# A layer-norm, attention and MLP kernel: the first 512 tokens of its head worked in two halves, and one V tile's products placed on both sides of the next chunk's transposes

## The chip, the cores and the metric

The kernel runs on one core of one Trainium2 chip. The metric is the device time of one launch in microseconds (us), as the median of several runs.

## What is computed

The input x has 2048 tokens of 512 features. It is layer-normed, and two branches read the result: attention with 32 heads of 16, and a gated MLP of inner width 1376.

```python
xn = _layernorm(x, axis=-1)                     # (x - mean) / sqrt(var + 1e-5)
qkv = xn @ wqkv                                 # q, k, v of 32 heads of 16
s = softmax(q @ k.T * 16 ** -0.5) @ v @ wo      # by head
g = silu(gelu(xn @ w1 + b1) @ w2 + b2)
return x + s * g
```

Each float32 operand of a product is split into a high part, rounded to the type that TensorE (PE) reads, and a low part, the rest. A product is the sum of three: high by high, high by low and low by high.

## The kernel before

The tokens are 16 tiles of 128 and 4 chunks of 512 (`NT`, `NCH`, `CH`); the features are 4 blocks of 128 (`KT`). The instructions of each engine stand in the order in which the Python code issues them (`manual_schedule`); each engine works its own list in order and waits for the others by semaphores. So the order of the code is the order of work, and an instruction that waits holds back all that stand behind it on its engine.

The part of the program that concerns us is its head, which prepares the operands. For a chunk, `ln` calls three steps on VectorE (DVE): `moments` of each tile (statistics and their aggregate, L414 and L415), `rstd` of the chunk (epsilon L419, the square root on ScalarE (ACT) at L420, the reciprocal and one refining step L421 to L424), and `norm` of each tile (L428), which also asks for the x tile six places on. `turn` transposes a normed tile on PE (L437, four blocks into one PSUM bank), and `split` takes the bank apart: ACT writes the high part (L86), DVE the low part (L87). The high and low parts of x lie in `slot0` and `slot1` for chunk 0, `slot2` and `slot3` for chunk 1, and so on.

`q_first(c)` makes the q and k rows of the first two head groups for a chunk: 24 products of 512 columns (L455) in two groups of accumulation, each in a bank of its own. They go term by term (high by high, then high weight by low x, then low weight by high x), and within each term first group 0, then group 1. `evac` then copies both banks (ACT, L370), splits them (ACT L374, POOL L375) and writes them to scratch memory. `v_tile(t)` makes the V rows of one token tile with 12 products (L92 by way of `mm3`), and `v_out` copies them into `vsb` on ACT (L387). V's weights are split on ACT (`wv_h`, L511) and POOL (`wv_low`, L502). Before the second pair of low halves, POOL waits in `pool_after` (L499) for a given normed tile.

Banks come from `a_tile`, which counts its calls and hands out six in turn: `ps_b`, `ps_x`, two of `spare` (shown as `sp`), `ps_t` (shown as `pst`) and `ps_a`. All of `ps_a`, `ps_b` and `ps_x` are shown as `ps`. A bank taken for the second time makes PE wait until whatever read its former contents is done.

The order of the head's code is: 25 warming products of the identity (`keep_warm`, L487), moments, root and norms of chunk 0, the split of the q and k weights (`w_split`, L294 on ACT, L295 on POOL), the transposes of tiles 0 to 3, `q_first(0)`; and then for each chunk c from 1: the transposes of its four tiles, `ln` of chunk c + 1, `v_tile(c - 1)` and `q_first(c)`. `ln` of chunk 1 is issued ahead of `q_first(0)`. Since `ln` of chunk c + 1 is issued ahead of `v_tile(c - 1)`, its square root stands on ACT ahead of that tile's `v_out`.

Behind the head come the MLP with the scores for the row maxima and then the attention itself (its first products with V in the chain of waits are at 484.65 us); their order is fixed as well.

Of the kernel before, what the change touches and what calls it, by code (L numbers as in the profile page):

```python
# [16 lines left out]
P = 128  # L17
S = 2048
D = 512
H = 32  # L20
DH = 16
KT = D // P
NT = S // P
CH = 512
# [30 lines left out]
def fused(ctx: ExitStack, tc: tile.TileContext, x, wqk, wv, wo, w1, b1, w2, b2, out):  # L55
# [308 lines left out]
    def evac(us, ph):  # L364
        raws = [wk.tile([P, CH], F32, name="hg", bufs=2) for u in us]
        for u, raw in zip(us, raws):
            if u[0] == "m":
                nc.scalar.activation(raw, ph.pop(u), AF.Gelu_apprx_tanh, bias=b1_sb[:, u[2]:u[2] + 1])  # L368
            else:
                nc.scalar.activation(raw, ph.pop(u), AF.Copy)  # L370
        for u, raw in zip(us, raws):
            hh = wk.tile([P, CH], F32R, name="hh", bufs=HB)
            hl = wk.tile([P, CH], F32R, name="hl", bufs=HB)
            nc.scalar.activation(hh, raw, AF.Copy)  # L374
            nc.gpsimd.tensor_sub(hl, raw, hh.bitcast(F32))  # L375
            if u[0] == "m":
                HS[u[1:]] = (hh, hl)
            else:
                rs, cs = slice(u[1] * P, (u[1] + 1) * P), slice(u[2] * CH, (u[2] + 1) * CH)
                nc.sync.dma_start(qk_h[rs, cs], hh.bitcast(F32))  # L380
                nc.sync.dma_start(qk_l[rs, cs], hl.bitcast(F32))
# [3 lines left out]
    def v_out(t, pv):  # L385
        dst = vsb[:, t, :H * VW].rearrange("p (h w) -> p h w", w=VW)[:, :, :DH]
        nc.scalar.activation(dst, pv.rearrange("p (h w) -> p h w", w=DH), AF.Copy)  # L387

    with ExitStack() as s1:
# [4 lines left out]
        def a_tile(shape):  # L394
            banks[0] += 1
            i = banks[0] % 6
            if i < 3:
                return (ps_a, ps_b, ps_x)[i].tile(list(shape), F32, name="ps")
            return f_bank(shape)
# [12 lines left out]
        def moments(t):  # L412
            st = w1k.tile([P, 6], F32, name="st")
            nc.vector.bn_stats(st, xs[t])  # L414
            nc.vector.bn_aggr(mv[:, t, :], st)  # L415

        def rstd(t0, t1):
            v = ve[:, :, t0:t1]
            nc.vector.tensor_scalar(v[:, 0], mv[:, t0:t1, 1], EPS, None, op0=OP.add)  # L419
            nc.scalar.activation(v[:, 1], v[:, 0], AF.Sqrt)  # L420
            nc.vector.reciprocal(v[:, 2], v[:, 1])  # L421
            nc.vector.scalar_tensor_tensor(v[:, 3], v[:, 2], -0.5, v[:, 2], op0=OP.mult, op1=OP.mult)
            nc.vector.tensor_mul(v[:, 3], v[:, 3], v[:, 0])
            nc.vector.scalar_tensor_tensor(v[:, 4], v[:, 3], 1.5, v[:, 2], op0=OP.add, op1=OP.mult)  # L424
# [8 lines left out]
        def turn(t):  # L433
# [4 lines left out]
            c, ts = t // NCH, slice(t % NCH * P, t % NCH * P + P)  # L438
            split(xh[c][:, :, ts], xl[c][:, :, ts], pt)

        def v_tile(t):
            pv = a_tile((P, D))
            c, ts = t // NCH, slice(t % NCH * P, t % NCH * P + P)
            for k in range(KT):
                mm3(pv, (xh[c][:, k, ts], xl[c][:, k, ts]), (wv_h[:, k], wv_l[:, k]), k == 0, k == KT - 1)
            v_out(t, pv)

        def q_first(c):
            pq = {}
            for n, (i, j) in enumerate(((0, 0), (0, 1), (1, 0))):  # L450
                for g in range(2):
                    if n == 0:
                        pq["q", g, c] = a_tile((P, CH))
                    for k in range(KT):
                        nc.tensor.matmul(pq["q", g, c], W1[g][i][:, k * P:(k + 1) * P], (xh, xl)[j][c][:, k],  # L455
                                         start=n == 0 and k == 0, stop=n == 2 and k == KT - 1)
            evac(list(pq), pq)

        for t in range(4):
            load_x(t, (nc.sync, nc.scalar)[t % 2])  # L460
# [24 lines left out]
        def keep_warm(n):  # L485
            for _ in range(n):
                nc.tensor.matmul(pw[:, :P], ident, ident, start=True, stop=True)  # L487

        keep_warm(25)
        def ln(t, n):  # L490
            for i in range(t, t + n):
                moments(i)
            rstd(t, t + n)
            for i in range(t, t + n):
                norm(i)

        ln(0, NCH)
        def pool_after(t):
            nc.gpsimd.tensor_sub(warm[:, :1], xns[t][:1, :1], xns[t][:1, :1])  # L499

        def wv_low(k):
            nc.gpsimd.tensor_sub(wv_l[:, k], wv_r[:, k], wv_h[:, k].bitcast(F32))  # L502

        pool_after(NCH - 1)
        for g in range(2):
            W1[g] = w_split(W1[g], "w1", 4)
        for t in range(NCH):
            turn(t)
        keep_warm(3)
        for k in range(KT):  # L510
            nc.scalar.activation(wv_h[:, k], wv_r[:, k], AF.Copy)  # L511
        for k in range(KT - 2):
# [3 lines left out]
        pool_after(2 * NCH - 1)  # L516
        for k in range(KT - 2, KT):
            wv_low(k)
        q_first(0)
        for c in range(1, NCH):  # L520
            for t in range(NCH * c, NCH * c + NCH):
                turn(t)
            if c < NCH - 1:
                ln(NCH * c + NCH, NCH)
            else:
                nc.scalar.activation(warm[:, 1:], warm[:, :1], AF.Gelu_apprx_tanh)
                break
            v_tile(c - 1)
            q_first(c)

    keep_r = ctx.enter_context(tc.tile_pool(name="keep_r", bufs=1, side="right"))
# [549 lines left out]
```

## Time and profile before

| | |
|---|---|
| median of 3 runs | 1546.86 us (1546.65 to 1547.5) |
| profiled execution | 1546.35 us, span 1544.6 us |
| busy PE / DVE / ACT / POOL | 100% / 92% / 78% / 24% |
| granted clock of PE | 1.00 |
| first statistics on DVE | 3.89 us |
| first q, k products on PE | 11.94 us |
| first transposes of chunk 1 | 18.11 us |
| q, k products of chunk 1 begin | 22.74 us |
| first transposes of chunk 2 | 28.34 us |
| first product of the MLP part | 51.49 us |

Times in the table's lower half are counted from the start of the span. In a timeline each row is a run of like instructions on one engine: start, length, engine, line, what is written from what, shapes and count, and in brackets how long the engine stood idle just before and which engine's work ended that. PE's products overlap, so the length of a row of products holds the tail of the last; the pace is read from start to start.

### The profile page before, as it was taken

How to read it: one execution, taken by the hardware profiler on the slowest of the kernel's cores; microseconds unless marked ns; L12 is line 12 of the kernel's file. 1: busy time of each engine (PE TensorE's matmuls, PEld its weight loads, DVE VectorE, ACT ScalarE, POOL GpSimd, SP SyncE). 2: the span in 40 equal slices, each digit the busy share in tenths (PEclk: the TensorE clock that was granted, in tenths of full speed). 3: DMA queues.
4: the chain of work that ended last, by engine and by line, in shares of the span. 5: the costliest groups of instructions: out<-in, count | busy, mean ns of one | idle time of the engine just before them, and what ended most of it. 6: DMA issues, size and time to landing. Idle time of an engine off the chain costs nothing.

```text
span 1544.6 us, 31302 instructions
## 1 busy us (share of the span) xinstructions
PE 1538.4 (100%) x12230; PEld 922.5 (60%) x12230; DVE 1419.2 (92%) x2294; ACT 1212.4 (78%) x1881; POOL 375.8 (24%) x386
## 2 busy tenths in 40 slices
PE   9999999999999999999999999999999999999998
PEld 8899999999995444444444444444444444444456
DVE  7799999999998999999999999999999999999945
ACT  4333433333339999999999999999999999999994
POOL 4235575756741011001000100100010000000153
PEclk9999999999999999999999999999999999999999
DMA  6615443455422112112411411411051111110162
GB/s 212 155 58 145 124 143 108 120 161 136 141 90 66 39 45 61 33 37 51 75 28 33 71 33 41 60 44 29 21 84 29 32 32 30 41 32 20 50 217 100
DMA packets 78227, 116.83 MB, mean 76 GB/s; under 512 B 28132, under 2 KB 28388, under 8 KB 76904
## 3 DMA queue, kind: packets, MB, share of 16 engines
q1 hardware_dynamic: 73596, 99.80, 23.1%
q0 software_dynamic: 4000, 14.45, 5.0%
q8 instruction: 96, 1.57, 0.4%
q10 hardware_dynamic: 484, 0.60, 0.1%
q14 instruction: 51, 0.42, 0.1%
HBM read 84.35 MB, written 25.97 MB: 71 GB/s over the span
## 4 chain that ended last, share of the span: by engine, by line
PE 99%; DVE 1%; DMA 0%; issue 0%; ACT 0%; DVEq 0%
PE pv L787 33%; PE ps L193 22%; PE ps L583 13%; PE two L716 8%; PE sp L583 5%; PE ps L716 4%; PE pst L716 4%; PE pst L583 3%; PE pv L583 2%; PE ps L916 2%; PE ps L92 1%; PE ps L455 1%; PE pst L92 0%; DVE st L414 0%; PE two L92 0%; DMA xt<-in_x 0%
## 5 line engine op out<-in xcount | busy, mean ns | idle before, releaser
L199 DVE TENSOR_REDUCE mx<-ps 128x2 f32<-128x512 f32 x2048 | 1318.0, 687 | 68.5 <-PE ps L193 18.3
L787 PE MATMUL pv<-slot,vsb 128*32 128x512 f32 x4096 | 543.4, 604 | 0.0
L721 ACT ACTIVATE slot<-two 128x1024 f32<-128x1024 f32 x511 | 520.5, 1019 | 0.0
L193 PEld LDWEIGHTS ps<-kt,slot 48*128 48x128 f32 x1356 | 212.2, 184 | 290.2 <-DVE mx L199 278.4
L193 PE MATMUL ps<-kt,slot 48*128 48x256 f32 (+1 forms) x1356 | 376.3, 366 | 0.0
L719 ACT ACTIVATE slot<-ps 128x512 f32<-128x512 f32 x515 | 307.5, 598 | 16.7 <-PE ps L716 7.2
L719 ACT ACTIVATE slot<-pst 128x512 f32<-128x512 f32 x511 | 309.9, 606 | 0.0
L583 PE MATMUL ps<-slot,w1h 64*128 64x512 f32 x1088 | 225.4, 392 | 0.0
L193 PE MATMUL ps<-kt,qz 48*128 48x512 f32 x512 | 202.2, 395 | 0.0
L716 PE MATMUL two<-qt,kt 50*128 50x512 f32 x766 | 197.5, 395 | 0.3 <-DVE gt L643 0.3
L716 PE MATMUL ps<-qt,kt 50*128 50x512 f32 x387 | 189.7, 492 | 0.0
L193 PEld LDWEIGHTS ps<-slot,slot 48*128 48x128 f32 x590 | 92.8, 184 | 124.0 <-DVE mx L199 118.2
L193 PE MATMUL ps<-slot,slot 48*128 48x256 f32 (+1 forms) x590 | 165.8, 366 | 0.0
L787 PEld LDWEIGHTS pv<-slot,vsb 128*32 128x32 f32 x4096 | 81.5, 108 | 131.9 <-issue 124.4
L583 PEld LDWEIGHTS ps<-slot,w1h 64*128 64x128 f32 x1088 | 154.1, 185 | 9.8
L583 PE MATMUL ps<-slot,w1l 64*128 64x512 f32 x544 | 157.0, 392 | 0.0
L716 PE MATMUL pst<-qt,kt 50*128 50x512 f32 x383 | 155.7, 406 | 0.0
L375 POOL TENSOR_TENSOR hl<-hg,hh 128x512 fp32r<-128x512 f32 x76 | 96.7, 1295 | 158.2 <-ACT hh L374 109.3
L368 ACT ACTIVATE hg<-ps,b_sb 128x512 f32<-128x512 f32 x44 | 27.9, 684 | 133.0 <-PE ps L583 121.7
L716 PEld LDWEIGHTS two<-qt,kt 50*128 50x128 f32 x766 | 114.5, 186 | 1.1 <-DVE gt L643 0.7
L246 POOL CAST mh<-nt 128x32 fp32r<-128x32 f32 x19 | 4.0, 209 | 375.7 <-DVE nt L244 322.8
L193 PEld LDWEIGHTS ps<-kt,qz 48*128 48x128 f32 x512 | 93.7, 183 | 1.0 <-DVE mx L199 0.7
(197 smaller groups left out, 1974.6 us busy)
## 6 DMA issues: line engine op xcount, KB each, us to landing
raw<-in_w SPq DMA_DIRECT2D x88, 256.0 KB
qk_h<-hh SPq DMA_DIRECT2D x32, 256.0 KB
qk_l<-hl SPq DMA_DIRECT2D x32, 256.0 KB
qt<-qk_h SPq DMA_DIRECT2D x128, 64.0 KB
slot<-qk_h SPq DMA_DIRECT2D x92, 64.0 KB
g_d<-gt POOLq DMA_DIRECT2D x16, 256.0 KB, 3.3
qt<-qk_l SPq DMA_DIRECT2D x64, 64.0 KB
dn<-den_d SPq DMA_DIRECT2D x32, 128.0 KB
```

Source lines behind the costliest of these rows:

```text
L92: nc.tensor.matmul(ps, lhs[a], rhs[b], start=first and n == 0, stop=last and n == 2)
L193: return nc.tensor.matmul(ps[:, c0:c0 + w], QS[u][r, p, qi * P:(qi + 1) * P], kts[u // NCH % KB][p][r, k0:k0 + w], start=True, stop=True).ins
L199: nc.vector.tensor_reduce(MX[u][:, 2 * p:2 * p + 2, qi, ki][:, heads, parts], ps.rearrange("p (n c) -> p n c", c=HC), axis=AX.X, op=OP.max)
L368: nc.scalar.activation(raw, ph.pop(u), AF.Gelu_apprx_tanh, bias=b1_sb[:, u[2]:u[2] + 1])
L375: nc.gpsimd.tensor_sub(hl, raw, hh.bitcast(F32))
L455: nc.tensor.matmul(pq["q", g, c], W1[g][i][:, k * P:(k + 1) * P], (xh, xl)[j][c][:, k], start=n == 0 and k == 0, stop=n == 2 and k == KT - 1)
L583: i = nc.tensor.matmul(ps, lhs[r], rhs[r], start=first, stop=last).ins
L716: nc.tensor.matmul(ps, kts[g % KB][p][r, k * P:(k + 1) * P], QT[u][r, p, :], start=True, stop=True)
L719: nc.scalar.activation(PT[u, k][:, 2 * p + a, :], ps, AF.Exp, scale=SCALE)
L721: nc.scalar.activation(PT[u, k][:, :2], TP["two"], AF.Exp, scale=SCALE)
L787: nc.tensor.matmul(PV[u][32 * j:32 * j + 32, :], vsb[:, k, h:h + 32], PT[u, k][:, j, :], start=(k == 0), stop=(k == NT - 1))
L916: HALF[0] = nc.tensor.matmul(PW[i][0], OTS[i, k][x][r], (wo_h, wo_l)[y][r, k], start=k == 0 and side == 0 and n == 0, stop=k == KT - 1 and ...
```

## The change

Chunk 0 is worked in halves of two tiles (256 tokens). `rstd` loses its first two instructions to a new `root`, so that the square root can be issued apart from what follows it. `q_first` becomes `q_part(c, c0, w)`, which makes w columns of a chunk's two banks and evacuates them when the last column is done; a half has 24 products of 256 columns. Chunks 1 to 3 call it with all 512. `v_tile(0)` is replaced by `v_terms`, which issues any of the three terms of a tile's V products, four each: eight (both terms with the high weight) now stand behind the second half of chunk 0, ahead of chunk 1's transposes, and the other four (low weight) where `v_tile(0)` stood. 20 warming products are left of 25, and POOL is let go for the weights' low halves after norm 1 instead of norm 3. The number of banks handed out stays the same, but V of tile 0 now takes its bank as the 7th call instead of the 11th.

The first place is DVE, from the norms of chunk 0 to the first statistics of chunk 1. `xn` is a normed tile, `st` a tile's statistics, `slot1` the low part of chunk 0; `xt_124`, `126`, `128` and `130` are token tiles 0 to 3, and `xt_139` is tile 4. Before:

```order
L428 TENSOR_SCALAR xn_197<-xt_124,mv_122,ve_123 128x512
L428 TENSOR_SCALAR xn_201<-xt_126,mv_122,ve_123 128x512
L428 TENSOR_SCALAR xn_205<-xt_128,mv_122,ve_123 128x512
L428 TENSOR_SCALAR xn_209<-xt_130,mv_122,ve_123 128x512
L87 TENSOR_TENSOR slot1_101<-ps_222,slot0_97 128x4x128
L87 TENSOR_TENSOR slot1_101<-ps_229,slot0_97 128x4x128
L87 TENSOR_TENSOR slot1_101<-sp_236,slot0_97 128x4x128
L87 TENSOR_TENSOR slot1_101<-sp_243,slot0_97 128x4x128
L414 BN_STATS st_259<-xt_139 128x6
```

Now, with the moments and epsilon of tile 3 and the second reciprocal and its refining in between:

```order
L431 TENSOR_SCALAR xn_189<-xt_124,mv_122,ve_123 128x512
L431 TENSOR_SCALAR xn_193<-xt_126,mv_122,ve_123 128x512
L414 BN_STATS st_206<-xt_130 128x6
L415 BN_AGGR mv_122<-st_206 128x2
L419 TENSOR_SCALAR ve_123<-mv_122 128x2
L87 TENSOR_TENSOR slot1_101<-ps_211,slot0_97 128x4x128
L87 TENSOR_TENSOR slot1_101<-ps_218,slot0_97 128x4x128
...
L431 TENSOR_SCALAR xn_258<-xt_128,mv_122,ve_123 128x512
L431 TENSOR_SCALAR xn_262<-xt_130,mv_122,ve_123 128x512
L87 TENSOR_TENSOR slot1_101<-pst_266,slot0_97 128x4x128
L87 TENSOR_TENSOR slot1_101<-ps_273,slot0_97 128x4x128
L414 BN_STATS st_286<-xt_139 128x6
```

The norms and the splits of tiles 2 and 3 have moved behind the splits of tiles 0 and 1, and the statistics of tile 4 stay behind all of them.

The second place is PE, from the end of chunk 0's q, k products to the start of chunk 1's (`kt1` holds V's weights here, `slot2` is chunk 1's high part, `w1h` and `w1l` are the weights of q and k). Before, with the repeating rows of V left out:

```order
L455 MATMUL ps_306<-slot0_97,w1l_219 128x512 x4
L437 MATMUL ps_343<-ident_120,xn_277 128x128 x4
L437 MATMUL ps_350<-ident_120,xn_281 128x128 x4
L437 MATMUL sp_357<-ident_120,xn_285 128x128 x4
L437 MATMUL sp_364<-ident_120,xn_289 128x128 x4
L92 MATMUL pst_401<-kt1_113,slot0_97 128x512 x2
L92 MATMUL pst_401<-kt1_113,slot1_101 128x512
...
L455 MATMUL ps_415<-slot2_98,w1h_214 128x512 x4
L455 MATMUL ps_420<-slot2_98,w1h_218 128x512 x4
```

Now:

```order
L473 MATMUL sp_233<-slot0_97,w1l_203 128x256 x4
L453 MATMUL ps_368<-kt1_113,slot0_97 128x512 x4
L453 MATMUL ps_368<-kt1_113,slot1_101 128x512 x4
L440 MATMUL ps_377<-ident_120,xn_304 128x128 x4
L440 MATMUL sp_384<-ident_120,xn_308 128x128 x4
L440 MATMUL sp_391<-ident_120,xn_312 128x128 x4
L440 MATMUL pst_398<-ident_120,xn_316 128x128 x4
L453 MATMUL ps_368<-kt1_113,slot0_97 128x512 x4
L473 MATMUL ps_440<-slot2_98,w1h_198 128x512 x4
L473 MATMUL ps_445<-slot2_98,w1h_202 128x512 x4
```

Eight V products have moved ahead of the four tiles' transposes and four stay behind them. V's bank, `ps_368`, is the 7th taken and is `ps_b`; chunk 1's second group, `ps_445`, is the 13th and is `ps_b` again.

The third place is ACT, from the first split of chunk 1 to the evacuation of its products, with the engines that each row waits for. Before:

```order
L86 ACTIVATE slot2_98<-ps_343 128x4x128 [waits PE_49]
L86 ACTIVATE slot2_98<-ps_350 128x4x128 [waits PE_49]
L86 ACTIVATE slot2_98<-sp_357 128x4x128 [waits PE_49]
L86 ACTIVATE slot2_98<-sp_364 128x4x128 [waits PE_49]
L420 ACTIVATE ve_123<-ve_123 128x4 [waits DVE_49]
L387 ACTIVATE vsb_90<-pst_401 128x32x16 [waits PE_49]
L370 ACTIVATE hg_441<-ps_415 128x512 [waits PE_49,Pool_49]
```

Now:

```order
L86 ACTIVATE slot2_98<-ps_377 128x4x128 [waits PE_49]
L86 ACTIVATE slot2_98<-sp_384 128x4x128 [waits PE_49]
L86 ACTIVATE slot2_98<-sp_391 128x4x128 [waits PE_49]
L86 ACTIVATE slot2_98<-pst_398 128x4x128 [waits PE_49]
L420 ACTIVATE ve_123<-ve_123 128x4 [waits DVE_49]
L387 ACTIVATE vsb_90<-ps_368 128x32x16 [waits PE_49]
L370 ACTIVATE hg_466<-ps_440 128x512 [waits PE_49,Pool_49]
```

The order is the same, the square root (L420) ahead of the V output (L387), but V now comes out of `ps_368` instead of `pst_401`. On PE, the rows that follow chunk 1's transposes now wait so:

```order
L453 MATMUL ps_368<-kt1_113,slot0_97 128x512 [waits Pool_49] x4
L473 MATMUL ps_440<-slot2_98,w1h_198 128x512 [waits Activation_49]
L473 MATMUL ps_440<-slot2_98,w1h_198 128x512 x3
L473 MATMUL ps_445<-slot2_98,w1h_202 128x512 [waits Activation_49]
L473 MATMUL ps_445<-slot2_98,w1h_202 128x512 x3
L473 MATMUL ps_440<-slot3_102,w1h_198 128x512 [waits DVE_49]
```

The first product into `ps_445` waits for ACT; before, its counterpart waited for DVE.

The diff:

```diff
--- before.py
+++ after.py
@@ -414,10 +414,13 @@
             nc.vector.bn_stats(st, xs[t])
             nc.vector.bn_aggr(mv[:, t, :], st)
 
-        def rstd(t0, t1):
+        def root(t0, t1):
             v = ve[:, :, t0:t1]
             nc.vector.tensor_scalar(v[:, 0], mv[:, t0:t1, 1], EPS, None, op0=OP.add)
             nc.scalar.activation(v[:, 1], v[:, 0], AF.Sqrt)
+
+        def rstd(t0, t1):
+            v = ve[:, :, t0:t1]
             nc.vector.reciprocal(v[:, 2], v[:, 1])
             nc.vector.scalar_tensor_tensor(v[:, 3], v[:, 2], -0.5, v[:, 2], op0=OP.mult, op1=OP.mult)
             nc.vector.tensor_mul(v[:, 3], v[:, 3], v[:, 0])
@@ -438,6 +441,20 @@
             c, ts = t // NCH, slice(t % NCH * P, t % NCH * P + P)
             split(xh[c][:, :, ts], xl[c][:, :, ts], pt)
 
+        pvs = {}
+
+        def v_terms(t, ns):
+            if t not in pvs:
+                pvs[t] = a_tile((P, D))
+            c, ts = t // NCH, slice(t % NCH * P, t % NCH * P + P)
+            for n in ns:
+                i, j = ((0, 0), (1, 0), (0, 1))[n]
+                for k in range(KT):
+                    nc.tensor.matmul(pvs[t], (xh, xl)[i][c][:, k, ts], (wv_h, wv_l)[j][:, k],
+                                     start=n == 0 and k == 0, stop=n == 2 and k == KT - 1)
+            if 2 in ns:
+                v_out(t, pvs.pop(t))
+
         def v_tile(t):
             pv = a_tile((P, D))
             c, ts = t // NCH, slice(t % NCH * P, t % NCH * P + P)
@@ -445,16 +462,22 @@
                 mm3(pv, (xh[c][:, k, ts], xl[c][:, k, ts]), (wv_h[:, k], wv_l[:, k]), k == 0, k == KT - 1)
             v_out(t, pv)
 
-        def q_first(c):
-            pq = {}
+        pq = {}
+
+        def q_part(c, c0, w):
             for n, (i, j) in enumerate(((0, 0), (0, 1), (1, 0))):
                 for g in range(2):
-                    if n == 0:
+                    if ("q", g, c) not in pq:
                         pq["q", g, c] = a_tile((P, CH))
                     for k in range(KT):
-                        nc.tensor.matmul(pq["q", g, c], W1[g][i][:, k * P:(k + 1) * P], (xh, xl)[j][c][:, k],
+                        nc.tensor.matmul(pq["q", g, c][:, c0:c0 + w], W1[g][i][:, k * P:(k + 1) * P],
+                                         (xh, xl)[j][c][:, k, c0:c0 + w],
                                          start=n == 0 and k == 0, stop=n == 2 and k == KT - 1)
-            evac(list(pq), pq)
+            if c0 + w == CH:
+                evac(list(pq), pq)
+
+        def q_first(c):
+            q_part(c, 0, CH)
 
         for t in range(4):
             load_x(t, (nc.sync, nc.scalar)[t % 2])
@@ -486,27 +509,42 @@
             for _ in range(n):
                 nc.tensor.matmul(pw[:, :P], ident, ident, start=True, stop=True)
 
-        keep_warm(25)
         def ln(t, n):
             for i in range(t, t + n):
                 moments(i)
+            root(t, t + n)
             rstd(t, t + n)
             for i in range(t, t + n):
                 norm(i)
 
-        ln(0, NCH)
         def pool_after(t):
             nc.gpsimd.tensor_sub(warm[:, :1], xns[t][:1, :1], xns[t][:1, :1])
 
         def wv_low(k):
             nc.gpsimd.tensor_sub(wv_l[:, k], wv_r[:, k], wv_h[:, k].bitcast(F32))
 
-        pool_after(NCH - 1)
+        keep_warm(20)
+        moments(0)
+        moments(1)
+        root(0, 2)
+        moments(2)
+        rstd(0, 2)
+        norm(0)
+        norm(1)
+        pool_after(1)
         for g in range(2):
             W1[g] = w_split(W1[g], "w1", 4)
-        for t in range(NCH):
+        moments(3)
+        root(2, 4)
+        for t in range(2):
             turn(t)
         keep_warm(3)
+        q_part(0, 0, HC)
+        rstd(2, 4)
+        norm(2)
+        norm(3)
+        for t in range(2, 4):
+            turn(t)
         for k in range(KT):
             nc.scalar.activation(wv_h[:, k], wv_r[:, k], AF.Copy)
         for k in range(KT - 2):
@@ -516,7 +554,8 @@
         pool_after(2 * NCH - 1)
         for k in range(KT - 2, KT):
             wv_low(k)
-        q_first(0)
+        q_part(0, HC, HC)
+        v_terms(0, (0, 1))
         for c in range(1, NCH):
             for t in range(NCH * c, NCH * c + NCH):
                 turn(t)
@@ -525,7 +564,10 @@
             else:
                 nc.scalar.activation(warm[:, 1:], warm[:, :1], AF.Gelu_apprx_tanh)
                 break
-            v_tile(c - 1)
+            if c == 1:
+                v_terms(0, (2,))
+            else:
+                v_tile(c - 1)
             q_first(c)
 
     keep_r = ctx.enter_context(tc.tile_pool(name="keep_r", bufs=1, side="right"))
```

## The prediction

> **What bounds the kernel now.** I began with the page: the busy shares and the chain that ended last.
>
> ```profile
> PE 1538.4 (100%) x12230; PEld 922.5 (60%) x12230; DVE 1419.2 (92%) x2294; ACT 1212.4 (78%) x1881; POOL 375.8 (24%) x386
> PE 99%; DVE 1%; DMA 0%; issue 0%; ACT 0%; DVEq 0%
> ```
>
> PE is on the chain for 99% of the span, so the end moves when PE is held up or relieved. Next came the table by stretches, to see whether something behind the head could swallow a shift. Its columns are length, busy time by engine with instruction counts, granted clock, DMA share and GB/s.
>
> ```profile
> core 0: us, PE busy (x) PEld busy (x) DVE busy (x) ACT busy (x) POOL busy (x), PEclk, DMA share, GB/s
> 30.00:50.00 20.00, 20.00 (x98) 16.31 (x96) 10.79 (x25) 10.76 (x22) 5.00 (x6) 1.00 0.58 154
> 50.00:450.00 400.00, 400.00 (x3417) 372.73 (x3416) 387.21 (x579) 139.85 (x253) 231.09 (x197) 1.00 0.44 126
> 550.00:1450.00 900.00, 900.00 (x7080) 401.14 (x7078) 852.44 (x1409) 889.51 (x1334) 76.96 (x114) 1.00 0.20 41
> ```
>
> From 30 us on PE never stands idle for long, and where it is held back (busy PE records contain such waits) DVE works 97% (387 of 400 us) and ACT 99% (890 of 900 us) of the stretch. Each of these engines starts its main work only behind the head and has no slack to give back. So I price the change by one number: how much later or earlier the q, k products of chunk 1 end, that is, when PE starts on chunk 2's transposes. What happens there passes to the end one for one.
>
> Third, the timeline of the head. Columns are start, length, engine, line, tiles, count, and in brackets the idle time ahead and its releaser.
>
> ```profile
> 3.89 0.69 DVE L414 BATCH_NORM_STATS2 st<-xt 128x6 f32<-128x512 f32 x1 [3.04 <-DMA xt<-in_x]
> 4.72 0.66 DVE L414 BATCH_NORM_STATS2 st<-xt 128x6 f32<-128x512 f32 x1
> 6.37 0.66 DVE L414 BATCH_NORM_STATS2 st<-xt 128x6 f32<-128x512 f32 x1
> 7.28 0.17 DVE L419 TENSOR_SCALAR ve<-mv 128x4 f32<-128x4 f32 x1
> 7.48 0.20 ACT L420 ACTIVATE ve<-ve 128x4 f32<-128x4 f32 x1 [4.32 <-DVE ve L419]
> 7.72 0.18 DVE L421 RECIPROCAL ve<-ve 128x4 f32<-128x4 f32 x1 [0.27 <-ACT ve L420]
> 7.86 1.33 ACT L294 ACTIVATE w1h<-raw 128x512 fp32r<-128x512 f32 x2 [0.18 <-DMA raw<-in_wqk]
> 8.53 1.92 DVE L428 TENSOR_SCALAR xn<-xt,mv,ve 128x512 f32<-128x512 f32 x4
> ...
> 9.13 1.11 PE L437 MATMUL ps<-ident,xn 128*128 128x128 f32 x8 [0.22 <-DVE xn L428]
> 9.82 1.08 ACT L86 ACTIVATE slot<-ps 128x512 fp32r<-128x512 f32 x2 [0.63 <-PE ps L437]
> ...
> 10.45 1.29 DVE L87 TENSOR_TENSOR slot<-ps,slot 128x512 fp32r<-128x512 f32 x2
> ...
> 10.79 1.09 ACT L86 ACTIVATE slot<-sp 128x512 fp32r<-128x512 f32 x2
> ...
> 11.74 2.21 ACT L511 ACTIVATE kt<-wv_r 128x512 fp32r<-128x512 f32 x4
> ...
> 11.94 1.19 PE L455 MATMUL pst<-slot,w1h 128*128 128x512 f32 x4
> ...
> 12.85 0.68 DVE L414 BATCH_NORM_STATS2 st<-xt 128x6 f32<-128x512 f32 x1
> ```
>
> Before 11.94 the bound is DVE's chain of four moments, root and norms, then the last tile's transposes and split. The steps I take from here: a tile's moments 0.83 us (4.72 less 3.89); last statistics to the epsilon line L419 0.91; L419 to the square root on ACT 0.20; reciprocal to first norm 0.81 (8.53 less 7.72); norms 0.46 apart (1.92 less one of 0.54, over three); first norm to transposes 0.60; transposes to split 0.69; L86 splits 0.49 apart; L86 start to its L87 0.63; last L86 start (10.79 + 0.49 = 11.28) to PE's products 0.66; four L87 to the next moments 2.40 (12.85 less 10.45), so 0.60 each.
>
> The next rows are the rest of the head, to the point where I measure.
>
> ```profile
> 16.17 0.17 DVE L419 TENSOR_SCALAR ve<-mv 128x4 f32<-128x4 f32 x1
> ...
> 17.42 1.92 DVE L428 TENSOR_SCALAR xn<-xt,mv,ve 128x512 f32<-128x512 f32 x4
> ...
> 18.11 1.09 PE L437 MATMUL ps<-ident,xn 128*128 128x128 f32 x8 [0.32 <-DVE xn L428]
> ...
> 19.42 0.18 POOL L499 TENSOR_TENSOR warm<-xn 1x1 f32<-1x1 f32 x1 [1.28 <-DVE xn L428]
> 19.57 2.55 POOL L502 TENSOR_TENSOR kt<-wv_r,kt 128x512 fp32r<-128x512 f32 x2
> ...
> 22.39 0.68 DVE L414 BATCH_NORM_STATS2 st<-xt 128x6 f32<-128x512 f32 x1
> ...
> 22.74 3.89 PE L455 MATMUL ps<-slot,w1h 128*128 128x512 f32 x16
> ...
> 25.71 0.17 DVE L419 TENSOR_SCALAR ve<-mv 128x4 f32<-128x4 f32 x1
> 25.91 0.21 ACT L420 ACTIVATE ve<-ve 128x4 f32<-128x4 f32 x1 [4.50 <-DVE ve L419]
> 26.03 0.58 ACT L387 ACTIVATE vsb<-pst 128x512 f32<-128x512 f32 x1
> ...
> 28.34 0.60 PE L437 MATMUL ps<-ident,xn 128*128 128x128 f32 x4
> ```
>
> The square root of tiles 8 to 11 (L420, 25.91) holds ACT idle for 4.50 us, and the V output of tile 0 (L387, 26.03) leaves directly behind it although its products are long done. Nobody waits for that copy now: PE runs chunk 1's products straight through, from 22.74 to the transposes at 28.34.
>
> **The change part by part.** For the length of products I need two more rows, the first and last of 24 products of 256 columns at the kernel's end, and the chain's row of 24 products of 512.
>
> ```profile
> 1537.68 0.28 PE L92 MATMUL ps<-wo_h,oh 128*128 128x256 f32 x1
> ...
> 1540.40 0.28 PE L92 MATMUL two<-wo_h,slot 128*128 128x256 f32 x1
> ```
>
> ```profile
> 22.90 5.60 PE ps L455 x24
> ```
>
> That is 2.72/23 = 0.118 us for 256 columns and 5.60/24 = 0.233 for 512: two halves of 24 cost 2 x 2.84 against 5.60, which is +0.08. I take the weight loads as hidden, as they are at the end. The five dropped warming products cost nothing: they would stand ahead of a wait for the first norm. The extra small DVE steps (a second set of five on two columns) are a few tenths on DVE and are in the sums below.
>
> *Start, tiles 0 and 1.* Two moments end in L419 at 4.72 + 0.91 = 5.63. The third tile's moments fill the wait for the root; reciprocal 6.62, first norm 7.43, second 7.89. Moments of tile 3 follow at 8.35, their L419 at 9.26 and the second root on ACT at 9.46. That root stands on ACT ahead of the splits, and ACT goes on 0.12 later (25.91 to 26.03), so tile 0's split leaves at 9.58, not at 7.43 + 0.60 + 0.69 = 8.72; tile 1's at 10.07. First products: 10.07 + 0.66 = 10.73, against 11.94. **Term 1: 1.21 earlier.** The weight splits (L294 ends 9.19) are in time. POOL's two low halves of the weights, let go after norm 1 instead of norm 3, take some 2.55 (the row at 19.57 has two of that size) and are done near 11.2, before the products that read them.
>
> *The second half.* 2.84 of products run to 13.57; norms 2 and 3 hide beneath them (L87 of tile 0 at 9.58 + 0.63 = 10.21, two of 0.60, reciprocal to norm 0.81: 12.22 and 12.68). But tiles 2 and 3 are turned only now: split of tile 2 at 13.57 + 0.69 = 14.26, of tile 3 at 14.75, products again at 15.41. In the 1.84 between, PE has two tiles of transposes (the row at 9.13 has two in 1.11) and idles for the rest, 0.73. The second half ends at 18.25 and eight V products (1.87) at 20.12.
>
> *What DVE does meanwhile.* It waits for these splits: L87 of tile 2 at 14.26 + 0.63 = 14.89, and moments of tiles 4 to 7 two L87 later, 16.09 against 12.85. **Term 2: DVE 3.24 late.** The norms go from 17.42 to 20.66 and the transposes from 18.11 to 21.35, so PE idles 1.2 where its row had a wait of 0.32. Early V products cover part of this wait, not all.
>
> *The V products that stay behind.* Their last two wait for POOL's low halves, which wait for norm 7: 19.42 + 3.24 = 22.66, halves done 2.70 later (19.57 + 2.55 less 19.42), at 25.36. PE is through with tile 0's V near 25.65 and starts chunk 1's products there instead of at 22.74: +2.9 if nothing else came.
>
> *The bank.* The row order puts V of tile 0 in the bank that the second group of chunk 1's products takes next; the bank before that change was released by an L87. Now it is released by the V output, and that copy stands on ACT behind the root of tiles 8 to 11, which DVE feeds last of all: four norms from 20.66 (1.92, to 22.58), four L87 (2.40), so the moments of tiles 8 to 11 begin at 24.98 instead of 22.39, +2.59. The root goes from 25.91 to 28.50, the copy runs from 28.62 to 29.20, and PE enters the second group 0.07 later (as 11.94 follows the end of the split, 10.79 + 1.08), at 29.27, with four products done and 20 left. 20 x 0.233 = 4.67, so the transposes of chunk 2 start at 33.94 against 28.34. **Sum: +5.6 us.** Queued behind the waiting product on PE is everything else; ACT's next copies wait for PE in turn. DVE has by then finished its norms for chunk 2 (29.6 to 31.5), so nothing is later still: from here the order of all engines is that of before.
>
> The wait's bounds from rows: nothing beyond +2.9 if the copy got out ahead of the root; and +6.1 if each of DVE's sixteen large steps between 16.1 and 28.3 took 0.03 longer, the spread of its statistics' rows (0.66 to 0.69). I keep the sum, since every step of that chain is a row of this kernel in the same order.
>
> The profiled execution took 1546.35 us with a span of 1544.6; the median shown is 1546.86. 1546.35 + 5.6 = 1551.95, and by the median 1552.5; I say 1552.3, which is 5.6 on a base of 1546.7.
>
> *PE's clock.* The sum makes PE idle twice in a row, 23.6 to 25.4 and 26.6 to 29.3, with six products between. In the head's first microseconds the same warming product ran slowly and then fast:
>
> ```profile
> 1.36 7.54 PE L487 MATMUL pv<-ident 128*128 128x128 f32 x50 [1.36 <-POOL ident masks.py:199]
> ```
>
> ```profile
> 2.00:4.00 2.00, 2.00 (x11) 2.00 (x11) 0.11 (x1) 1.15 (x2) 0.44 (x2) 1.00 0.97 330
> 4.00:6.00 2.00, 2.00 (x16) 2.00 (x15) 1.93 (x5) 0.00 (x0) 0.00 (x0) 1.00 0.97 313
> 6.00:8.00 2.00, 2.00 (x21) 2.00 (x20) 1.59 (x7) 0.34 (x2) 0.00 (x0) 1.00 0.96 329
> ```
>
> 11 records in 2 us at first and 21 later, at a granted clock of 1.00 in both; the 16 between put the switch near 5.0. [...]
>
> **The rivals.**
>
> First, *the copy is no brake*: the second group finds its bank free, as now. For it speaks that the copy is only 0.58 long and that its products end well ahead of the root; against it, that ACT runs in order and that L387 follows L420 by 0.12 in the trace. Then only +2.9 is left: 1546.7 + 2.9 = 1549.6.
>
> Second, *PE slows after the pauses*. At half rate for as long as in the head (1.36 to about 5.0, 3.6 us) PE would do half of its products there, so 1.8 is added: 1552.3 + 1.8 = 1554.1. [...]
>
> Third, the one on the other side, *the early start is kept*. If DVE's moments of tiles 4 to 7 did not wait for the second half, PE would run on from 10.73: 5.68 of products, 1.11 for two tiles' transposes, and 4.63 for the other four tiles and V (18.11 to 22.74), to 22.15, or 22.88 with the idle 0.73 between the halves. That is -0.6 to +0.1 against 22.74: 1546.1 to 1546.8. It decides if norm 4 can start by 19.4; DVE's order forbids it, since two L87 of the second half stand ahead of the moments.
>
> **How the numbers follow.** Forecast (1551 to 1553.3) 0.74; PE slows 0.10; no brake 0.09; early start kept 0.05; 0.02 for what I don't see. 0.2% is 3.1 us, about what a measurement of this kernel can tell from no change, so slower begins at 1550.0: forecast, slow PE and half of the unseen give 0.86 with a little of the second case; within 0.2% 0.13; faster 0.01, since the most that could be gained is 0.6. The range reaches from the case without a brake to the slow clock: 1549.3 to 1554.5.
>
> **What would show it.** In the changed profile: first 256-column products near 10.7; a split of tile 0 right behind a root of two columns at 9.5; moments of tiles 4 to 7 at 16; transposes of tile 4 near 21.3; an ACT copy to vsb at 28.7 behind a root at 28.5; a PE wait of over 2 us for ACT inside chunk 1's products; and the transposes of chunk 2 near 34. If the second group starts next to the first, the bank term was wrong. If moments of tile 4 start by 13, term 2 was. If the shift at 34 us isn't found again at the end, some engine did have slack behind the head.

## The result: 8.3 us slower

The changed kernel takes 1555.09 us (median of 6 runs, 1554.32 to 1555.77) against 1546.76 (1546.46 to 1547.78) before: a ratio of 1.0052, with a 95% interval of 1.0039 to 1.0065. Slower was right. The size was not: 5.6 us were forecast, 8.3 were measured, and 1555.09 lies above the range's end of 1554.5. The six runs fall into two groups, 1554.32 to 1554.53 and 1555.64 to 1555.77, and the median lies between them. The profiled execution took 1554.53 us, with a span of 1552.7 against 1544.6.

The page of the changed kernel, its busy shares and the chain:

```profile
PE 1540.9 (99%) x12244; PEld 925.7 (60%) x12244; DVE 1420.7 (91%) x2299; ACT 1212.2 (78%) x1882; POOL 375.5 (24%) x386
PE 98%; DVE 1%; ACT 0%; DMA 0%; issue 0%; DVEq 0%
```

PE is still the chain, with 98% where it had 99%. The timeline of the changed kernel's head follows (lines have moved: norms L431, transposes L440, q and k products L473, V of tile 0 L453):

```profile
8.63 2.49 POOL L295 TENSOR_TENSOR w1l<-raw,w1h 128x512 fp32r<-128x512 f32 x2
...
9.18 0.74 DVE L419 TENSOR_SCALAR ve<-mv 128x2 f32<-128x2 f32 x1
...
9.96 0.20 ACT L420 ACTIVATE ve<-ve 128x2 f32<-128x2 f32 x1 [1.50 <-DVE ve L419]
10.06 1.06 ACT L86 ACTIVATE slot<-ps 128x512 fp32r<-128x512 f32 x2
...
11.18 2.10 PE L473 MATMUL sp<-slot,w1h 128*128 128x256 f32 x16 [0.85 <-ACT slot L86]
...
15.81 2.15 PE L473 MATMUL sp<-slot,w1h 128*128 128x256 f32 x16 [0.74 <-ACT slot L86]
...
16.50 0.68 DVE L414 BATCH_NORM_STATS2 st<-xt 128x6 f32<-128x512 f32 x1
...
21.16 1.92 DVE L431 TENSOR_SCALAR xn<-xt,mv,ve 128x512 f32<-128x512 f32 x4
...
21.86 0.63 PE L440 MATMUL ps<-ident,xn 128*128 128x128 f32 x4 [1.10 <-DVE xn L431]
...
26.22 1.08 PE L473 MATMUL ps<-slot,w1h 128*128 128x512 f32 x4
...
29.07 0.20 ACT L420 ACTIVATE ve<-ve 128x4 f32<-128x4 f32 x1 [4.49 <-DVE ve L419]
29.19 0.58 ACT L387 ACTIVATE vsb<-ps 128x512 f32<-128x512 f32 x1
...
29.82 4.56 PE L473 MATMUL ps<-slot,w1h 128*128 128x512 f32 x12 [2.52 <-ACT vsb L387]
...
36.11 0.60 PE L440 MATMUL ps<-ident,xn 128*128 128x128 f32 x4
```

Read it against the forecast: first products 11.18 (forecast 10.73, before 11.94); moments of tile 4 at 16.50 (16.09, before 12.85); transposes of tile 4 at 21.86 (21.35, before 18.11); root and V copy at 29.07 and 29.19 (28.50 and 28.62); the second group at 29.82 behind a wait of 2.52 us for ACT (29.27). Up to here everything is as forecast and half a microsecond late. Then the 20 products left, which were to take 4.67 us, take 6.29, from 29.82 to the transposes of chunk 2 at 36.11. The table by stretches of the changed kernel shows why (length, busy time by engine, granted clock third from the right):

```profile
core 0: us, PE busy (x) PEld busy (x) DVE busy (x) ACT busy (x) POOL busy (x), PEclk, DMA share, GB/s
28.00:30.00 2.00, 0.18 (x1) 0.18 (x2) 1.56 (x8) 0.69 (x2) 0.30 (x1) 1.00 1.03 361
30.00:32.00 2.00, 2.00 (x7) 1.58 (x8) 1.96 (x5) 0.00 (x0) 0.00 (x0) 0.74 0.17 43
32.00:34.00 2.00, 2.00 (x6) 1.59 (x5) 0.03 (x1) 0.00 (x0) 0.00 (x0) 0.50 0.69 262
34.00:36.00 2.00, 2.00 (x9) 1.61 (x9) 0.00 (x0) 0.55 (x1) 0.00 (x0) 0.91 0.00 0
```

PE ran at half of its clock from 30.9 to 34.3 us (0.74 over 30 to 32 is 1.0 us at half, 0.91 over 34 to 36 is 0.4). That costs 1.6 us. Chunk 2 is 36.11 - 28.34 = 7.77 us late, and the first MLP product, at 59.23 against 51.49, 7.74 us.

### The profile page after: what moved, and what is told of

It reads as the page before. It is cut to its first block, busy times and chain, and to the rows that moved or that the text cites. A ratio compares the mean times of both kernels' runs of the same rounds, so it can differ in the third digit from the quotient of the medians.

```text
span 1552.7 us, 31332 instructions
## 1 busy us (share of the span) xinstructions
PE 1540.9 (99%) x12244; PEld 925.7 (60%) x12244; DVE 1420.7 (91%) x2299; ACT 1212.2 (78%) x1882; POOL 375.5 (24%) x386
## 4 chain that ended last, share of the span: by engine, by line
PE 98%; DVE 1%; ACT 0%; DMA 0%; issue 0%; DVEq 0%
PE pv L829 33%; PE ps L193 21%; PE ps L625 13%; PE two L758 8%; PE sp L625 5%; PE pst L758 5%; PE ps L758 4%; PE pst L625 3%; PE pv L625 2%; PE ps L958 2%; PE ps L92 1%; PE ps L473 1%; DVE st L414 0%; PE sp L473 0%; PE two L92 0%; DVE slot L87 0%
## 5 line engine op out<-in xcount | busy, mean ns | idle before, releaser
L368 ACT ACTIVATE hg<-ps,b_sb 128x512 f32<-128x512 f32 x44 | 27.9, 685 | 136.1 <-PE ps L625 118.0
```

## The experiments

My theory after the result had three parts: the shared bank makes PE wait for the V copy behind the root (the forecast); the pause lowers PE's clock; POOL's subtraction, let go early, holds up DVE's epsilon step L419 (0.74 us instead of 0.17 at 9.18; POOL's two subtractions take 2.49 from 8.63, so the first ends near 9.88, and L419 ends at 9.92). The main rival was that DVE's lateness alone accounts for it all, whatever the bank. Ratios are against the kernel before on the same chip (median 1546.66 for the half-filled pause, the version with the gates back and the repeat; 1546.85 for the halves and V apart and for the reordered version; 1546.62 for the others).

### V in a bank of its own

```diff
-                pvs[t] = a_tile((P, D))
+                banks[0] += 1
+                pvs[t] = ps_m.tile([P, D], F32, name="ps")
```

> The changed kernel with V of tile 0 in a bank of its own that nothing else takes in the head, the count of the other banks kept. Theory (bank, then clock): the second group of chunk 1's products starts right behind the first, PE has no pause of 2.5 us, its granted clock stays 1.00 from 20 to 36 us, and chunk 2's transposes start at 26.22 + 5.60 = 31.8 us instead of 36.1; the time falls from 1555.1 to about 1550.3, still 3.5 above before. Rival (DVE's lateness alone costs it all, the bank is innocent): the second group still waits, 1555.1.

Measured: 1550.15 us, ratio 1.0023 (1.0014 to 1.0032). PE's and ACT's rows of this kernel:

```profile
26.43 3.90 PE L474 MATMUL ps<-slot,w1h 128*128 128x512 f32 x16
...
32.03 0.60 PE L440 MATMUL ps<-ident,xn 128*128 128x128 f32 x4
```

```profile
29.30 0.21 ACT L420 ACTIVATE ve<-ve 128x4 f32<-128x4 f32 x1 [4.49 <-DVE ve L419]
29.41 0.58 ACT L387 ACTIVATE vsb<-ps 128x512 f32<-128x512 f32 x1
```

The copy leaves as late as ever, behind its root, but nobody waits for it: products run on, chunk 2 starts at 32.03 at full clock. The changed kernel is 8.5 us above the 1546.62 of these runs; of that the bank and what hangs on it cost 4.9, and 3.5 remain.

### The V copy ahead of the root

```diff
+            if c == 1:
+                v_terms(0, (2,))
             if c < NCH - 1:
                 ln(NCH * c + NCH, NCH)
...
-            if c == 1:
-                v_terms(0, (2,))
-            else:
+            if c > 1:
                 v_tile(c - 1)
```

> The changed kernel with the last four V products of tile 0, and so the V output on ACT, issued ahead of the moments and the root of tiles 8 to 11; the bank stays shared. Theory: the bank costs nothing when the copy does not stand behind the root on ACT; the copy runs near 26.4 us, the second group starts by 27.2, chunk 2's transposes near 31.9, about 1550.4 us. Rival (sharing the bank is dear in itself, whatever the order): second group at 29 or later, 1553 to 1555.

Measured: 1550.25 us, ratio 1.0023 (1.0014 to 1.0032). ACT and PE of this kernel, in one timeline:

```profile
27.03 0.60 ACT L387 ACTIVATE vsb<-ps 128x512 f32<-128x512 f32 x1 [1.85 <-PE ps L453]
...
29.67 0.21 ACT L420 ACTIVATE ve<-ve 128x4 f32<-128x4 f32 x1 [2.04 <-DVE ve L419]
...
32.46 0.60 PE L440 MATMUL ps<-ident,xn 128*128 128x128 f32 x4
```

The bank is shared, the copy leaves 2.64 us ahead of the root, and the time is that of a bank of its own. (This execution's first x tile came at 4.54, 0.6 later than the changed kernel's, which is why its rows are later than expected.) So neither the shared bank nor the copy is dear by itself. It takes both: a bank that the next products need, and a copy that stands behind a step that waits for DVE.

### The pause filled

```diff
+                    if c == 1 and n == g == 0:
+                        keep_warm(11)
```

> The changed kernel with eleven warming products (identity by identity, into the bank of the other warming products) between the two groups of chunk 1's products, where PE stood idle for 2.5 us. The wait for the V output stays. Theory (the pause lowers the clock): granted clock 1.00 from 28 to 36 us, the second group still starts at 29.8, chunk 2's transposes at 29.82 + 4.67 = 34.5 instead of 36.1, and the time is 1.6 to 2.9 lower than the changed kernel's 1555.1: 1552.2 to 1553.5. Rival (the lower clock comes from something else, such as the power drawn or the start of the span): clock 0.5 again near 31 to 34 us, 1555 or a little more.

Measured: 1553.01 us, ratio 1.0040 (1.0028 to 1.0053). PE's timeline and the stretches of this kernel:

```profile
27.58 2.62 PE L512 MATMUL pv<-ident 128*128 128x128 f32 x22
30.25 3.07 PE L473 MATMUL ps<-slot,w1h 128*128 128x512 f32 x12
...
35.02 0.60 PE L440 MATMUL ps<-ident,xn 128*128 128x128 f32 x4
```

```profile
30.00:32.00 2.00, 1.94 (x10) 1.43 (x9) 1.90 (x7) 0.20 (x1) 0.00 (x0) 1.00 0.41 95
32.00:34.00 2.00, 2.00 (x10) 1.64 (x9) 0.47 (x2) 0.00 (x0) 0.00 (x0) 1.00 0.67 255
```

Each warming product counts as two records, so x22 are the eleven. The second group has to wait just as long for the copy, but the clock stays at 1.00, 20 products take 4.77 us (30.25 to 35.02) instead of 6.29, and 2.1 us are gone. Eleven products of no use make the kernel faster. That it was the pause that lowered the clock is shown.

### The pause half filled

The same edit with `keep_warm(5)`.

> The changed kernel with five warming products in the pause instead of eleven, so that about 1.4 us of the pause is left idle. [...]

Measured: 1553.08 us, ratio 1.0041 (1.0028 to 1.0055). PE and one stretch of it:

```profile
27.48 1.27 PE L512 MATMUL pv<-ident 128*128 128x128 f32 x10
30.16 3.06 PE L473 MATMUL ps<-slot,w1h 128*128 128x512 f32 x12 [1.40 <-ACT vsb L387]
```

```profile
30.00:32.00 2.00, 1.84 (x8) 1.53 (x9) 1.90 (x7) 0.11 (x1) 0.00 (x0) 1.00 0.36 80
```

A wait of 1.40 us left the clock at 1.00 here (from 26 to 36 us); one of 2.52 was followed by half clock. The time expected was that of eleven products, 1553.0, and 1554.5 or more had the clock fallen here too.

### POOL let go later

```diff
-        pool_after(1)
...
         moments(3)
         root(2, 4)
+        nc.gpsimd.tensor_sub(warm[:, :1], ve[:1, 0, 2:3], ve[:1, 0, 2:3])
+        for g in range(2):
+            nc.gpsimd.tensor_sub(W1[g][1], raws[g], W1[g][0].bitcast(F32))
```

> The changed kernel with POOL let go for the low halves of the q, k weights only after DVE's epsilon step for tiles 2 and 3 (L419), not after norm 1. Theory (the step of 0.74 us at 9.18 waited for POOL's subtraction beside it): that step takes 0.17 us, the second root starts near 9.4 instead of 9.96, the first products near 10.6 instead of 11.18, and all that follows is some 0.5 earlier: 1554.5. Rival (the step was slow for its own reasons, or the start is not what sets the rest): 0.74 again, or 1555.1 in spite of 0.17.

Measured: 1553.66 us, ratio 1.0046 (1.0034 to 1.0059). The timeline of this kernel's start, and PE's row of chunk 2:

```profile
9.23 0.17 DVE L419 TENSOR_SCALAR ve<-mv 128x2 f32<-128x2 f32 x1
9.44 0.20 ACT L420 ACTIVATE ve<-ve 128x2 f32<-128x2 f32 x1 [0.63 <-DVE ve L419]
...
10.66 1.53 PE L473 MATMUL sp<-slot,w1h 128*128 128x256 f32 x11 [0.70 <-ACT slot L86]
```

```profile
35.60 0.60 PE L440 MATMUL ps<-ident,xn 128*128 128x128 f32 x4
```

L419 takes 0.17, the first products come 0.52 earlier and chunk 2 0.51. The clock falls here too, after a wait of 2.50 us (0.54 over 30 to 32, 0.60 over 32 to 34). The medians differ by 1.4, more than the profiles. Part of that is the two groups of the changed kernel: four of the five runs here lie at 1553.56 to 1553.66, which is 0.8 below its lower group. The other 0.3 is open.

### The two halves of the change apart

Halves alone, with V of tile 0 whole in its old place:

```diff
-        v_terms(0, (0, 1))
...
-            if c == 1:
-                v_terms(0, (2,))
-            else:
-                v_tile(c - 1)
+            v_tile(c - 1)
```

> The changed kernel with V of tile 0 whole where it stood before, behind the transposes of chunk 1 and in its old bank (the 11th taken); only the halves are left of the change. Theory (halves make DVE late, and a long pause lowers PE's clock): PE stands idle from the end of the second half, near 18.7, to the transposes at 21.9, 3.2 us; V ends near 26.4, no wait for a bank follows. Chunk 2's transposes at 26.4 + 5.6 = 32.0 at full clock, or 33.6 with one window at half clock, which I expect after a pause of 3.2 us: 1552.0 us (1550.3 if the clock holds). Rival (the halves gain and the V split alone loses): below 1547.

Measured: 1552.63 us, ratio 1.0038 (1.0024 to 1.0051). PE and the stretches of this kernel:

```profile
22.08 1.94 PE L440 MATMUL ps<-ident,xn 128*128 128x128 f32 x8 [2.96 <-DVE xn L431]
...
35.02 0.60 PE L440 MATMUL ps<-ident,xn 128*128 128x128 f32 x4
```

```profile
22.00:24.00 2.00, 1.92 (x9) 1.95 (x10) 1.47 (x4) 1.16 (x3) 0.61 (x2) 0.50 0.68 153
24.00:26.00 2.00, 2.00 (x11) 1.90 (x10) 1.68 (x3) 1.43 (x3) 2.00 (x2) 0.50 0.76 263
26.00:28.00 2.00, 2.00 (x6) 1.61 (x5) 1.80 (x5) 0.37 (x1) 2.00 (x3) 0.52 0.91 347
```

PE waits 2.96 us for norm 4; the clock falls near 21.1, within the wait, and stays at half until 27.9: 6.8 us, twice the 3.4 us of the changed kernel, which were expected. That is why chunk 2 comes at 35.02, not at 33.6. This was the longest of the four runs, 1553.55 us at a mean clock of 0.997. The other three, 1551.92 to 1552.80 us at 0.999, came nearer to the 1552.0 expected, so the doubled length of the half clock probably belongs to this execution alone. Without the halves, and with V split (`v_terms` as in the changed kernel) in the bank that comes next:

```diff
         q_first(0)
+        v_terms(0, (0, 1))
...
-            v_tile(c - 1)
+            if c == 1:
+                v_terms(0, (2,))
+            else:
+                v_tile(c - 1)
```

> The kernel before with only the V products of tile 0 split, eight ahead of chunk 1's transposes and four behind, the bank taken as it comes (the 7th). Theory (bank): the second group of chunk 1's products waits for the copy behind the root of tiles 8 to 11 here too; root near 26.3, second group near 27.1, a pause of 3.7 us from 23.4, and a window at half clock behind it: chunk 2's transposes near 31.7 + 1.6 = 33.3, 1551.7 us. Rival (the bank waits only because the halves make DVE late): the second group starts by 24, 1546.5.

Measured: 1552.63 us, ratio 1.0038 (1.0024 to 1.0051). PE of this kernel:

```profile
27.59 4.61 PE L469 MATMUL ps<-slot,w1h 128*128 128x512 f32 x12 [3.86 <-ACT vsb L387]
...
33.91 0.60 PE L437 MATMUL ps<-ident,xn 128*128 128x128 f32 x4
```

A wait of 3.86 us for the V copy, and 20 products in 6.32 us behind it, since the clock is 0.65 over 28 to 30 us and 0.50 over 30 to 32. Each part alone loses 6 us by a wait of its own. Together they lose 8.3, less than the sum: V's eight products fill part of the wait for norm 4, which is 1.10 us in the changed kernel instead of 2.96, and the wait for the copy is 2.52 instead of 3.86.

V split, with V in a bank of its own:

> The same, with V of tile 0 in a bank of its own. Theory: the eight products fill the wait for norm 4, POOL's last low half (22.1 us) then holds the last V product, chunk 1's products start near 22.4 instead of 22.74: 0.3 below before, 1546.3. Rival (V's split costs something of itself): above before by 0.5 or more.

Measured: 1547.19 us, ratio 1.0002 (0.9993 to 1.0010): no gain. PE of this kernel:

```profile
23.04 3.88 PE L470 MATMUL ps<-slot,w1h 128*128 128x512 f32 x16
...
28.96 0.63 PE L437 MATMUL ps<-ident,xn 128*128 128x128 f32 x4 [0.18 <-DVE xn L428]
```

Chunk 1's products begin 0.3 earlier than before if one allows for the first x tile, which came at 4.51 here instead of 3.89 (23.04 - 0.62 = 22.42, against 22.74). But chunk 2's transposes then wait 0.18 for norm 8: 28.96 - 0.62 = 28.34, as before. The wait that V filled came back at DVE one chunk later.

### A version without the waits

Halves kept, the rest reordered. The core of the edit on the changed kernel:

```diff
-        pool_after(1)
...
+        eps(2, 4)
+        nc.gpsimd.tensor_sub(warm[:, :1], ve[:1, 0, 2:3], ve[:1, 0, 2:3])
         for t in range(2):
             turn(t)
+        sqrt(2, 4)
...
+        for k in range(KT):
+            nc.scalar.activation(wv_h[:, k], wv_r[:, k], AF.Copy)
         rstd(2, 4)
...
+        pool_after(3)
+        for k in range(KT):
+            wv_low(k)
+        moments(4)
+        moments(5)
         for t in range(2, 4):
             turn(t)
+        v_terms(0, (0,))
...
-        pool_after(2 * NCH - 1)
...
-        v_terms(0, (0, 1))
+        v_terms(0, (1, 2))
...
+            if c == 1:
+                v_terms(1, (0,))
...
+            if c == 2:
+                v_terms(1, (1, 2))
```

> Halves kept, the waits that the runs named taken away: V of tile 0 in a bank of its own and its copy ahead of the next root; POOL let go after the epsilon step of tiles 2 and 3; the second root on ACT behind the splits of tiles 0 and 1; the moments of tiles 4 and 5 in DVE's wait for the second half; V's weights split early; V products of tile 0 between the halves and of tile 1 behind chunk 1's transposes. Theory (the halves as such cost only the two late transposes, about what the early start gains): first products near 10.5, chunk 2's transposes 0.5 to 1.0 earlier than before with the four V products of tile 1 counted, 1545.6 to 1546.3. Rival (working in halves costs in itself): 1548 or more.

Measured: 1551.33 us, ratio 1.0030 (1.0019 to 1.0041), on the rival's side. I had taken away POOL's wait for norm 7, and its rows show what that wait was for:

```profile
10.03 2.55 POOL L551 TENSOR_TENSOR w1l<-raw,w1h 128x512 fp32r<-128x512 f32 x2
...
11.37 1.23 DVE L426 TENSOR_TENSOR ve<-ve 128x2 f32<-128x2 f32 x1
...
20.27 4.50 DVE L431 TENSOR_SCALAR xn<-xt,mv,ve 128x512 f32<-128x512 f32 x4
...
21.53 2.49 POOL L375 TENSOR_TENSOR hl<-hg,hh 128x512 fp32r<-128x512 f32 x2
```

Four norms take 4.50 us instead of 1.92 when POOL's two subtractions begin among them, and a step of 128x2 elements (L426, which takes 0.16 elsewhere) takes 1.23, to the end of POOL's subtraction at 12.58. So POOL's early work can cost DVE far more than the 0.57 us found above. PE waits for the held norms, and this row bears on the clock:

```profile
24.46 0.63 PE L440 MATMUL sp<-ident,xn 128*128 128x128 f32 x4 [2.41 <-DVE xn L431]
```

```profile
24.00:26.00 2.00, 1.54 (x11) 1.49 (x12) 2.00 (x5) 0.88 (x2) 0.02 (x1) 1.00 0.62 155
```

A wait of 2.41 us, hardly shorter than the 2.50 to 2.52 after which the clock fell elsewhere, left it at 1.00 in this execution. The other six runs of this kernel were 0.9 to 1.8 us longer, at mean clocks of 0.998 and 0.999; whether the clock fell in them isn't shown. With the gates back:

```diff
-        nc.gpsimd.tensor_sub(warm[:, :1], ve[:1, 0, 2:3], ve[:1, 0, 2:3])
+        pool_after(1)
...
         consts()
+        pool_after(7)
```

> The reordered kernel with POOL held back once more: its low halves of the q, k weights are let go by norm 1 as in the change, and its work behind the constants waits for norm 7. Theory (norms and POOL's subtractions shut each other out): the four norms of tiles 4 to 7 take 1.92 us again instead of 4.50, chunk 2's transposes come near 28.5 with four V products of tile 1 already done, and the time is 1546.0 (1545.6 to 1546.6). Rival (the halves cost in themselves): above 1547.

Measured: 1546.95 us, ratio 1.0002 (0.9993 to 1.0011).

```profile
17.67 0.80 DVE L419 TENSOR_SCALAR ve<-mv 128x4 f32<-128x4 f32 x1
...
19.55 1.96 DVE L431 TENSOR_SCALAR xn<-xt,mv,ve 128x512 f32<-128x512 f32 x4
...
29.40 0.63 PE L440 MATMUL ps<-ident,xn 128*128 128x128 f32 x4 [0.32 <-DVE xn L431]
```

This lies between the 1546.0 expected and the rival's 1547. The norms are back at 1.96 and 4.2 us are won (4.5 above the kernel before on its chip, now 0.3), but it is no faster than the kernel before: PE waits 0.32 for norm 8, since DVE is the bound again, and L419 of tiles 4 to 7 takes 0.80 beside POOL's subtractions (it ends at 18.47, they at 18.44). Taking off the 0.16 by which the first x tile was later (4.05 against 3.89) and 0.93 for four V products done early, chunk 2 starts at 28.31 where before it was 28.34. No version here beats the kernel before.

### The changed kernel once more

> The changed kernel once more, unaltered, for a second look at the clock: its runs fall into two groups, 1554.3 to 1554.5 and 1555.6 to 1555.8. Theory (a second window at half clock, or a longer one, in the upper group): a run of the upper group shows over 3.4 us of half clock, one of the lower group 3.4 us. Rival (the 1.2 us come from elsewhere): the same length of half clock in both.

One run, 1554.97 us, with the first x tile at 4.50 (0.57 later than in the first profile), half clock from 31.15 to 34.55 and chunk 2 at 36.70. It belongs to neither group. What sets the upper group apart stays open: its three runs show a mean granted clock of 0.998, the three of the lower group 0.999. Over a span of 1553 us that is about 3.1 and 1.6 us of clock lost, so a longer stretch at half clock, as the profile of the halves alone has it, is likely. But the last digit is weak evidence, since the kernel before shows 0.999 too, in runs of 1546.64 and 1546.83 us.

## Why the prediction was right and wrong

**That the end follows the head** held. From the first MLP product to the end of the span, all kernels take nearly the same:

| kernel | first MLP product, us | span, us | between, us |
|---|---|---|---|
| before | 51.49 | 1544.6 | 1493.1 |
| changed | 59.23 | 1552.7 | 1493.5 |
| own bank | 55.14 | 1548.3 | 1493.2 |
| pause filled | 58.18 | 1551.3 | 1493.1 |
| halves alone | 58.16 | 1551.7 | 1493.5 |
| V alone | 57.02 | 1550.4 | 1493.4 |

The changed kernel's row in its own profile, from a timeline behind the head:

```profile
59.23 0.49 PE L625 MATMUL pst<-kt,slot 64*128 64x512 f32 x1
```

In these six profiles nothing of a head's loss is given back in 1493 us.

**Term 1**, 1.21 us earlier, measured 0.76. The step that failed here is the sentence that POOL's low halves "are done near 11.2, before the products that read them": that was true (8.63 + 2.49 = 11.12), but the sum had no price for it on DVE. L419 ended at 9.92, with POOL's first subtraction (near 9.88); the second root stands behind L419 and the first splits behind the root. This is 0.5 us on everything. In the rows, DVE's steps beside POOL's subtractions took 0.74 us against 0.17 (L419), 1.23 against 0.16 (L426 of the reordered version) and 4.50 against 1.92 (its four norms); by what means POOL holds DVE they don't show.

**Term 2**, DVE 3.24 us late, measured 3.65 (16.50 - 12.85): right, with the 0.5 of term 1 in it.

**The bank** was right in mechanism and size: 2.7 us were forecast (5.6 less 2.9), and chunk 2 comes 4.08 us earlier with a bank of its own (32.03 against 36.11), of which 1.62 is clock, so 2.5. A bank of its own, or the copy ahead of the root, takes the wait away, and what is left, 3.5 us, is what the working called "+2.9 if nothing else came", with the 0.5 of term 1.

**PE's clock** is the term that failed by most: the sum put it at nothing, and the half clock was given 0.10. No run shows that pauses such as the sum had, 2.7 us the longest, cost no clock. What they show is half clock after a pause of 2.52 us, and after one of 2.51 in the second profile of this kernel. The clock fell 1.1 us after work had begun again in the first and 0.8 in the second, and stayed down for 3.4 us. 20 products took 1.62 us longer, where the rival had 1.8. Filled with products of no use, the pause cost no clock (1.00 from 26 to 36 us). The half clock lasted 3.4 us here and with V alone, 6.8 with the halves alone, and after 2.41 us in the reordered kernel's profile it did not come. Which pauses bring it, and what sets its length, is not shown.

The sum as it came out, in the profiles: 5.6 forecast, 0.55 from L419 (with 0.04 of a later first x tile), 1.62 from the clock: 7.77 at chunk 2. On the base of 1546.7 that is 1554.5, the very end of the range, which had been drawn to take in the slow clock. So the slow clock alone would have stayed inside it. The span is 8.1 longer, with 0.4 of it behind the first MLP product (1493.5 against 1493.1), and the median 8.3, since three of the six runs are of the upper group, whose cause is open.

**The early start kept** was rightly held unlikely. The reordered version with its gates back only breaks even, although PE waits there for no bank; it still waits 0.32 us for norm 8, and L419 still takes 0.80 us beside POOL. That the two late transposes and the second wait for their splits take back what the early start wins is argued, not shown.

## What to carry to other kernels

When an operation is moved, count the buffers too: which one it now takes, who has it next, and behind what its release stands in the releasing engine's queue. A head that starts earlier is worth nothing if the engine that feeds the next stage then waits for something later; follow that engine through one more stage. Price a pause of PE of some 2.5 us with its clock too (1.6 us here), and where it can't be avoided try a few products of no use in it: five were as good as eleven.

## What the runs showed of the hardware that I had not expected

- After waits of 2.52, 2.96 and 3.86 us PE's granted clock was at half for 3.4, 6.8 and 3.4 us; after 1.40 and, in one profile, 2.41 us it stayed at 1.00. In the first and the last case the fall came about 1 us after work had begun again; in the middle one it came within the wait, 1 us before its end. Why it stayed down twice as long there, no run shows.
- Two DVE steps on 128x2 elements, L419 of the changed kernel and L426 of the reordered one, took 0.74 and 1.23 us instead of 0.17 and 0.16 beside a POOL subtraction, and ended when that did (9.92 and 12.60, against some 9.88 and 12.58). Not every step is held: in the version with the gates back the statistics and splits that ran beside POOL's subtractions from 13.39 to 18.44 us kept their 0.66 to 0.69 us each.
- The first x tile lands between 3.89 and 4.54 us after the start of the span from one execution to the next, and the head moves with it. Rows of two profiles compare only to that, unless the difference is taken off.
